# Order of the first attention phase in a fused attention and two-FFN kernel: weight conversions, bias tables and reciprocal products placed behind the latest maximum

## The chip, the cores and the metric

One core of one Trainium2 chip runs the whole program. The metric is the device time of one execution in microseconds (us). Half a per cent of it is about 4.9 us. The engines have short names: PE is TensorE (PEld its weight loads), DVE is VectorE, ACT is ScalarE, POOL is GpSimd, SP is SyncE, whose queue issues every DMA here.

## The reference, cut to what matters

Attention over 4 batches, 8 heads, 576 positions, head dimension 64, with a causal mask and a bias from a running sum of `s`; then two feed-forward networks over the 2304 tokens. All data are float32, and the kernel keeps that precision by splitting operands into a high and a low part.

```python
scores = scale * np.matmul(q, k.transpose(0, 1, 3, 2))
cum = np.cumsum(np.maximum(s, 0.0), axis=-1)
bias = -(cum[:, :, :, None] - cum[:, :, None, :])
scores = np.where(causal, -1000000000.0, scores + np.minimum(bias, 0.0))
scores = scores - np.max(scores, axis=-1, keepdims=True)
attn = np.exp(scores)
attn = attn / (np.sum(attn, axis=-1, keepdims=True) + 1e-09)
x = np.matmul(attn, v)                      # then tokens x 512
h = x @ w_in;  x = (h - np.tanh(h)) @ w_out          # d_ff 2048
x = ((x @ w1) * (x @ w2) @ w3) @ w_out2              # d_ff 1024
```

## The kernel before, in words

The kernel has three phases. Only the first is touched: attention, with the first half of the first network (feature blocks 0 to 7) laid between its steps as filler for PE. The rest of the first network and the second network follow.

**Pairs and steps.** Attention works on pairs of heads. `Pair` objects are numbered in the order in which they run: p0 to p3 are the first 256 queries ("A") of batch 0's four head pairs, p4 to p7 the other 320 queries ("B") of the same; from p8 on come the batches 1 to 3. An A pair has one unit of work, a B pair has three (B1, B2, B3). A loop over steps `k`, from -2 on, calls what the table `when` holds for each step, in the order given by a small number; `at(k, order, fn)` fills the table (lines 486 to 513). Unit `j` of a pair scores at its step, takes its row maximum and its exponentials one step later, is transposed 5 (A of batch 0) or 7 steps later, and so on. p0, p1, p2, p3 score at steps 0, 2, 4, 6; p4 at 8, 10, 12, p5 at 14, 16, 18, and so on to p7 at 26, 28, 30; p8 at 32. In steps 0 to 11 three idle matmuls (`warm`, line 197) stand at each step.

**Batch 0.** Here the bias is added by PE: `scores` (line 208) follows the score matmuls with matmuls of two small tables, `rel0` and `rel1`, made by `relative` (line 568) on DVE from the running sum; five column ranges are made, for the five chunks of queries, and all five stand ahead of the first maximum. `minimum` (line 231) takes the row maxima on DVE (L241) and scales them by -0.125 (L245); `exps` (line 257) computes the exponentials on ACT from the PSUM banks (L270, L271). In unit B3 two chunks end: chunk 2 (all in B3's banks) and chunk 4 (512 columns in B2's banks, 64 in B3's), so B2's two banks stay taken until chunk 4 is through ACT.

**Banks.** Scores, transposes and products share a pool of five PSUM banks (`ps_a`). PE's order is the program's own (`manual_schedule`); a score matmul that finds no bank stops PE until ACT has read one.

**Products.** `invert` makes reciprocals of the row sums; they go by PE transpose (`turn`), ACT (`store`), a DMA to DRAM (L329) and two broadcast DMAs back (`spread`, L335) to a tile `rb`; `finish` (line 344) multiplies the attention product by it on DVE (L348) into `xy`, from which `xhl`, the network's input, is split by ACT (L63) and DVE (L64). The network's first block may start when p3 is finished: `fin` (line 510) is its step, 15 for p3.

**Weights.** Weight tiles arrive as 64-bit numbers and are turned to float32 by three DVE instructions (`plain`, lines 78 to 89: L82, L85, L87), split by ACT (L63) and POOL (L64). `conversions` (line 353) loads and converts them one after the other through two raw tiles; the first two loads are issued at the start, the first conversions stand in steps 0 and 3, later ones every 2.2 steps (line 601), and each from the third on waits for the latest score matmul (`after_pe`, a semaphore wait). `parked` (line 368) does the same from step 36 on for the other half of the weights.

**Order.** On DVE, ACT, POOL and SP each engine runs its instructions in one fixed order, which the scheduler of the framework sets from the program's order, priorities and its own timing model. So a wait of one instruction holds all behind it on the engine.

## Time and profile before

| | |
|---|---|
| median of 3 runs | 974.52 us (971.75 to 977.34) |
| profiled execution, its own time | 970.3 us |
| its span, first to last instruction | 968.5 us |
| mean granted PE clock | 0.989 |
| PE busy | 935.1 us (97%) |
| PEld / DVE / ACT / POOL busy | 808.1 / 558.3 / 418.3 / 258.3 us |
| PE idle in 0 to 60 us / after 340 us | 11.4 us / 11.8 us |

The busy table says how long each engine worked, not what set the end. The two rows on idle time are the lengths of those stretches less PE's busy time in them. The view of waits by engine, the timeline of one engine and the table of stretches with the granted clock tell where PE stood still, and at which clock it worked after.

### The profile page before, as it was taken

Reading aid. Unit: us, or ns where it says so; the run is one execution under the profiler, and the core shown is the slowest. Engines: PE = TensorE matmul, PEld = TensorE weight load, DVE = VectorE, ACT = ScalarE, POOL = GpSimd, SP = SyncE. Lnnn points to the kernel's source line nnn. Section 1 sums busy time; section 2 is a strip of 40 time slices with the busy share of each in tenths; the row PEclk is TensorE's granted clock in tenths of the full one; section 3 lists DMA queues with packets and bytes.
Section 4 is the critical chain, followed back from the end, with each engine's and each line's share of the span. In section 5 each row is a group of like instructions: output and inputs, shape, how many; then the busy total and the mean of one; then the engine's idle time right before and its main releaser. Section 6 shows DMA issues by size and latency. Waiting matters only on the chain.

```text
span 968.5 us, 16343 instructions
## 1 busy us (share of the span) xinstructions
PE 935.1 (97%) x5953; PEld 808.1 (83%) x5953; DVE 558.3 (58%) x1311; ACT 418.3 (43%) x1029; POOL 258.3 (27%) x254
## 2 busy tenths in 40 slices
PE   8799999899999999999999999989999999999997
PEld 4466776688788789998888888978899999999997
DVE  8565556677667776776977566785322712342221
ACT  4565777767676654333433333332222412331220
POOL 3123766455555510000000000023222501340220
PEclk9898999999999999999999999999999999999999
DMA  6544353554444522489573563484366737664611
GB/s 200 164 137 149 123 193 135 178 184 153 162 142 147 178 102 97 162 299 362 212 262 140 193 217 131 134 283 157 101 196 196 206 101 205 196 173 151 197 55 66
DMA packets 67711, 165.66 MB, mean 171 GB/s; under 512 B 7504, under 2 KB 22000, under 8 KB 65584
## 3 DMA queue, kind: packets, MB, share of 16 engines
q1 hardware_dynamic: 67632, 164.62, 51.7%
q8 instruction: 47, 0.77, 0.3%
q14 instruction: 32, 0.26, 0.1%
HBM read 127.74 MB, written 36.86 MB: 170 GB/s over the span
## 4 chain that ended last, share of the span: by engine, by line
PE 81%; DMA 3%; issue 3%; POOL 3%; DVE 2%; ACT 2%; SPq 0%; POOLq 0%; ACTq 0%; DVEq 0%
PE W L813 10%; PE hb L111 9%; PE yb L111 9%; PE h L111 9%; PE y L416 8%; PE o L829 5%; PE Y L813 5%; PE q L829 5%; PE w3o L111 5%; PE pv L311 4%; PE s_B L214 4%; PE pt_B L285 3%; PE V L813 2%; POOL pr L193 1%; DMA raw_w<-in_w3t 1%
## 5 line engine op out<-in xcount | busy, mean ns | idle before, releaser
L111 PEld LDWEIGHTS h<-xhl,win 128*128 128x128 f32 x864 | 107.0, 189 | 21.7 <-issue 10.7
L111 PE MATMUL h<-xhl,win 128*128 128x256 f32 x864 | 121.7, 287 | 1.3 <-DVE th L448 0.6
L111 PE MATMUL hb<-x,win 128*128 128x512 f32 (+1 forms) x480 | 104.6, 367 | 0.0
L111 PE MATMUL yb<-ghb,wout 128*128 128x512 f32 (+1 forms) x320 | 96.1, 367 | 0.4 <-ACT ghb L63 0.4
L111 PEld LDWEIGHTS hb<-x,win 128*128 128x128 f32 x480 | 83.9, 188 | 15.0
L193 POOL TENSOR_SCALAR pr<-cb,cq 128x384 f32<-128x384 f32 (+1 forms) x48 | 88.2, 1852 | 2.9 <-DMA cb<-cum_d 2.1
L416 PE MATMUL y<-gh,wout 128*128 128x256 f32 x576 | 86.8, 290 | 0.0
L274 ACT ACTIVATE pr<-pr,nm 128x128 f32<-128x128 f32 (+2 forms) x120 | 71.3, 596 | 22.4 <-DVE nm L252 21.8
L64 POOL TENSOR_TENSOR B11hl<-xy,B11hl 128x768 fp32r<-128x768 f32 x3 | 5.6, 1863 | 279.8 <-ACT B11hl L63 279.8
L416 PEld LDWEIGHTS y<-gh,wout 128*128 128x128 f32 x576 | 73.8, 191 | 5.2 <-issue 4.0
L885 POOL TENSOR_TENSOR c<-c,c 128x384 f32<-128x384 f32 x24 | 25.8, 1074 | 171.8 <-DVE c L869 171.8
L111 PEld LDWEIGHTS yb<-ghb,wout 128*128 128x128 f32 x320 | 58.2, 188 | 10.5 <-ACT ghb L63 0.6
L214 PE MATMUL s_B<-qk 64*96 64x512 f32 (+2 forms) x256 | 57.5, 513 | 9.4 <-ACT pr L270 6.8
L829 PE MATMUL o<-p,w3s 128*128 128x384 f32 x288 | 61.4, 335 | 1.0 <-ACT p L63 1.0
L111 PE MATMUL yb<-glb,wout 128*128 128x512 f32 (+1 forms) x160 | 58.5, 368 | 0.4 <-DVE glb L64 0.4
L252 DVE CUSTOM_DVE_ANT_0 pr<-s_B,pr 96x512 f32<-96x512 f32 (+1 forms) x72 | 44.9, 639 | 19.9 <-PE s_B L214 18.6
L285 PE MATMUL pt_B<-ident,pr 96*128 96x96 f32 (+1 forms) x384 | 52.5, 260 | 0.3 <-ACT pf_A L294 0.3
L829 PEld LDWEIGHTS o<-p,w3s 128*128 128x128 f32 x288 | 50.8, 188 | 1.5 <-ACT p L63 1.3
L829 PE MATMUL q<-p,w3s 128*128 128x384 f32 x288 | 50.9, 335 | 0.1
L829 PEld LDWEIGHTS q<-p,w3s 128*128 128x128 f32 x288 | 50.0, 188 | 0.4 <-DVE pp L882 0.4
L294 ACT COPY pf_B<-pt_B 128x512 f32<-128x512 f32 (+2 forms) x72 | 35.8, 497 | 30.3 <-PE pt_B L285 29.5
L416 PE MATMUL y<-gl,wout 128*128 128x256 f32 x288 | 45.7, 281 | 2.7 <-POOL gl L64 2.7
(169 smaller groups left out, 1871.8 us busy)
## 6 DMA issues: line engine op xcount, KB each, us to landing
S<-wg_d SPq DMA_DIRECT2D x96, 256.0 KB
A<-wg_d SPq DMA_DIRECT2D x72, 256.0 KB
qk<-in_qk SPq DMA_DIRECT2D x16, 576.0 KB
raw_win<-in_w_in SPq DMA_DIRECT2D x16, 512.0 KB
raw_wout<-in_w_out SPq DMA_DIRECT2D x16, 512.0 KB
raw_w<-in_w SPq DMA_DIRECT2D x16, 512.0 KB
wg_d<-pks SPq DMA_DIRECT2D x8, 1024.0 KB
raw_w<-in_w3t SPq DMA_DIRECT2D x16, 512.0 KB
```

The source lines that it names most:

```text
L111: i = nc.tensor.matmul(ps, a, b, start=first and n == 0, stop=last and n == 2, skip_group_check=skip)
L193: nc.gpsimd.tensor_scalar(out=t[:pw, e, :w], in0=p.cb[:pw, e, :w], scalar1=c, scalar2=0.0, op0=ALU.add, op1=ALU.min)
L214: latest[0] = nc.tensor.matmul(ps[e][:PW[i], o:o + k1 - k0], x[:, 0, CH0[i]:CH0[i] + PW[i]], x[:, 1, k0:k1], start=(i, k0, k1, o) == UNITS ...
L252: nc.vector.tensor_tensor_reduce(out=t[:pw, k0:k1], in0=ps[:pw, o:o + k1 - k0], in1=t[:pw, k0:k1], scale=-0.125, scalar=nm[:pw, 5:6] if k0 ...
L274: nc.scalar.activation(t[:pw, :], t[:pw, :], AF.Exp, bias=m, scale=-1.0, accum_out=p.sums[:pw, e, c:c + 1])
L285: nc.tensor.transpose(pt[:, at:at + pw], p.pr[i][:pw, e, KC0[kj]:KC0[kj] + P], ident[:pw, :pw])
L294: (nc.vector.tensor_copy if j == "B2" and not p.first else nc.scalar.copy)(pf[:, :at], pt[:, :at])
L311: nc.tensor.matmul(p.pv[D * e:D * e + D, c:p.nq], p.vs[:, e, kj], pf[:, beg:end], start=z == 0, stop=z == len(todo) - 1, skip_group_check= ...
L416: nc.tensor.matmul(o, wout[f][:, z, P * c:P * c + P], x, start=f == 0 and n == 0 and c % 2 == 0, stop=f == F1 - 1 and n == 2, skip_group_c ...
L813: nc.tensor.matmul(ps[:, :T], w[:, x, P * j:P * j + P], b[:, y, j], start=first and j == n == 0, stop=last and j == 1 and n == 2, skip_gro ...
L829: nc.tensor.matmul(os_[c][:, :T], w3s[f][:, a, P * c:P * c + P], p[:, b], start=f == 0 and n == 0, stop=f == NG - 1 and n == 2, skip_group ...
L885: nc.gpsimd.tensor_mul(c12, c12, c22)
```

## The change

It touches the first phase only.

1. `in_turn` is new: it orders an instruction behind another on the same engine, without a semaphore. `latest` remains the latest score matmul; the new `least` is the latest instruction of a row maximum (L249 of the new kernel, or the fused one for later batches).
2. The first DVE instruction of each conversion stands in turn behind `least`, and waits no more for a score matmul.
3. The first two raw loads are no longer issued at the start: `conversions` is first called at step 1, then every second step, 18 times to step 35; so loads are issued at steps 1 and 3, behind the latest score matmul, and the first two conversions stand at steps 5 and 7.
4. The bias tables are ordered behind `least`; the first two chunks' are still made before any maximum, the others now behind one.
5. The products of `finish` are ordered behind `least`; for A pairs of batch 0 they stand one step later (`fin` + 5), so the network's first block may start at step 16.
6. Where batch 0 takes maxima and exponentials, the chunks of a unit come in reverse: in B3 chunk 4 before chunk 2, in A chunk 1 before chunk 0.

```diff
+    def in_turn(i, behind):
+        if behind is not None:
+            tc.add_manual_dep(i.ins, behind.ins.name, mybir.DependencyInfo(mybir.DependencyClass.NoSync, mybir.DependencyReason.SCHED_ONLY))
...
-        after_pe(i, behind)
+        in_turn(i, behind)
...
-        latest, paces = [None], []
+        latest, least, paces = [None], [None], []
...
-                for i, k0, k1, o in UNITS[j]:
+                for i, k0, k1, o in reversed(UNITS[j]):
...
-                        nc.vector.tensor_scalar(out=nm[:pw, :, c:c + 1], in0=nm[:pw, :, c:c + 1], scalar1=-0.125, scalar2=None, op0=ALU.mult)
+                        least[0] = nc.vector.tensor_scalar(out=nm[:pw, :, c:c + 1], in0=nm[:pw, :, c:c + 1], scalar1=-0.125, scalar2=None, op0=ALU.mult)
...
-                    nc.vector.tensor_tensor_reduce(
+                    least[0] = nc.vector.tensor_tensor_reduce(
...
-            for i, k0, k1, o in UNITS[j]:
+            for i, k0, k1, o in reversed(UNITS[j]) if p.first else UNITS[j]:
...
-                    nc.vector.tensor_mul(xy[:, p.hp, c:c + z - q], p.pv[:, q - p.q0:z - p.q0], p.rb[:, r:r + z - q])
+                    in_turn(nc.vector.tensor_mul(xy[:, p.hp, c:c + z - q], p.pv[:, q - p.q0:z - p.q0], p.rb[:, r:r + z - q]), least[0])
...
-                raws.append(load_raw(*todo[m][2:], nc.sync if m < 2 else nc.scalar, pin=fs[0] == 0))
-                if m < 2:
-                    yield
+                raws.append(load_raw(*todo[m][2:], behind=latest[0]))
+                yield
...
-                d[f] = convert(raws.pop(0), n, behind=latest[0] if m > 1 else None)
+                d[f] = convert(raws.pop(0), n, behind=least[0])
...
-                park(raws.pop(0), n, wf_d[m], f2, latest[0])
+                park(raws.pop(0), n, wf_d[m], f2, least[0])
...
-            fin = ke + lag + (4 if p.first and p.early else 3)
+            fin = ke + lag + (5 if p.first and p.early else 3)
...
-        next(conv)
-        next(conv)
...
-            nc.vector.tensor_scalar(out=hi, in0=cum[:, :w], scalar1=base, scalar2=None, op0=ALU.subtract)
+            in_turn(nc.vector.tensor_scalar(out=hi, in0=cum[:, :w], scalar1=base, scalar2=None, op0=ALU.subtract), least[0])
...
-            if k >= 0 and convs < 2 * F1 and 5 * k >= 11 * convs:
+            if convs < 2 * F1 + 2 and k >= 1 + 2 * convs:
                 at(k, 5.8, next, conv, None)
                 convs += 1
-            if convs == 2 * F1 and k >= 36 and k % 6 == 0:
+            if convs == 2 * F1 + 2 and k >= 36 and k % 6 == 0:
```

What this does to the order of the engines is shown at three places. The number after a tile's name tells tiles of one kind apart; it is not the same in the two kernels.

DVE from the bias tables to the first maximum, before (`rel` are the tables, `cvt` the converted weights, `nm` the maxima of p0 and p1):

```order
L574 SCALAR_TENSOR_TENSOR rel_139<-cum,rel_139 32x512
L574 SCALAR_TENSOR_TENSOR rel_138<-cum,rel_138 32x576
L574 SCALAR_TENSOR_TENSOR rel_139<-cum,rel_139 32x384
L82 TENSOR_SCALAR cvt_win_179<-raw_win_126 128x512
L82 TENSOR_SCALAR cvt_wout_246<-raw_wout_128 128x512
L85 SCALAR_TENSOR_TENSOR cvt_win_179<-raw_win_126,cvt_win_179 128x512
L85 SCALAR_TENSOR_TENSOR cvt_wout_246<-raw_wout_128,cvt_wout_246 128x512
L87 SCALAR_TENSOR_TENSOR cvt_win_179<-raw_win_126,cvt_win_179 128x512
L87 SCALAR_TENSOR_TENSOR cvt_wout_246<-raw_wout_128,cvt_wout_246 128x512
L241 TENSOR_REDUCE nm_188<-s_A_162 128x1 x2
L241 TENSOR_REDUCE nm_188<-s_A_163 128x1 x2
```

The same place now (the lines are those of the changed kernel, L245 and L249 for the maximum):

```order
L574 TENSOR_SCALAR rel_134<-cum 32x128
L574 TENSOR_SCALAR rel_134<-cum 32x256
L575 SCALAR_TENSOR_TENSOR rel_134<-cum,rel_134 32x128
L575 SCALAR_TENSOR_TENSOR rel_134<-cum,rel_134 32x256
L245 TENSOR_REDUCE nm_175<-s_A_158 128x1 x2
L245 TENSOR_REDUCE nm_175<-s_A_159 128x1 x2
L249 TENSOR_SCALAR nm_175<-nm_175 128x2 x2
L574 TENSOR_SCALAR rel_135<-cum 32x512
L575 SCALAR_TENSOR_TENSOR rel_135<-cum,rel_135 32x512
```

Three of the five tables moved behind the first and the second maximum, and both conversions behind the third and the fourth.

DVE at the maxima of p4's unit B3, before (`xy<-pv_544` is the product of p3):

```order
L241 TENSOR_REDUCE nm_410<-s_B_0_510 128x1
L241 TENSOR_REDUCE nm_410<-s_B_0_510 96x1
L241 TENSOR_REDUCE nm_410<-s_B_1_511 128x1
L241 TENSOR_REDUCE nm_410<-s_B_1_511 96x1
L348 TENSOR_TENSOR xy<-pv_544,rb_507 128x256
L245 TENSOR_SCALAR nm_410<-nm_410 128x2
L243 TENSOR_TENSOR nm_410<-nm_410 96x2
L245 TENSOR_SCALAR nm_410<-nm_410 96x2
```

The same place now (`xy<-pv_473` is the product of p2; that of p3 comes ten rows further on):

```order
L245 TENSOR_REDUCE nm_392<-s_B_0_492 96x1
L245 TENSOR_REDUCE nm_392<-s_B_0_492 128x1
L245 TENSOR_REDUCE nm_392<-s_B_1_493 96x1
L245 TENSOR_REDUCE nm_392<-s_B_1_493 128x1
L247 TENSOR_TENSOR nm_392<-nm_392 96x2
L249 TENSOR_SCALAR nm_392<-nm_392 128x2
L86 TENSOR_SCALAR cvt_win_525<-raw_win_418 128x512
L249 TENSOR_SCALAR nm_392<-nm_392 96x2
L352 TENSOR_TENSOR xy<-pv_473,rb_439 128x256
```

The product of p3 no longer stands between the maxima and their scaling, but the first instruction of a conversion does.

ACT at the exponentials of p4's B3, before:

```order
L63 CAST xhl_2_592<-xy 128x256
L63 CAST xhl_3_595<-xy 128x256
L271 ACTIVATE pr_2_468,sums_425<-s_B_0_510,nm_410 128x384
L271 ACTIVATE pr_2_468,sums_425<-s_B_1_511,nm_410 128x384
L270 ACTIVATE pr_4_407,sums_425<-s_B_0_460,nm_410 96x512
L271 ACTIVATE pr_4_407,sums_425<-s_B_0_510,nm_410 96x64
L270 ACTIVATE pr_4_407,sums_425<-s_B_1_461,nm_410 96x512
```

The same place now:

```order
L274 ACTIVATE pr_4_389,sums_407<-s_B_0_442,nm_392 96x512
L275 ACTIVATE pr_4_389,sums_407<-s_B_0_492,nm_392 96x64
L274 ACTIVATE pr_4_389,sums_407<-s_B_1_443,nm_392 96x512
L275 ACTIVATE pr_4_389,sums_407<-s_B_1_493,nm_392 96x64
L275 ACTIVATE pr_2_450,sums_407<-s_B_0_492,nm_392 128x384
L275 ACTIVATE pr_2_450,sums_407<-s_B_1_493,nm_392 128x384
L63 CAST xhl_2_600<-xy 128x256
```

Chunk 4, which reads B2's banks, now comes ahead of chunk 2, and the split of `xhl`, which waits for the products, behind both.

On PE only the network's matmuls move: `h` of block 0, feature block 0, starts one step (16 for 15) later, and the units after it follow at the new spacing; the attention matmuls keep their order.

## Rows read from the trace of the kernel before

**Rows 1.** The page: span, and busy time of each engine.

```profile
span 968.5 us, 16343 instructions
...
PE 935.1 (97%) x5953; PEld 808.1 (83%) x5953; DVE 558.3 (58%) x1311; ACT 418.3 (43%) x1029; POOL 258.3 (27%) x254
```

**Rows 2.** PE's timeline (start, duration, instruction xcount [idle before <-releaser]).

```profile
9.05 0.23 PE L229 MATMUL s_A<-maskb,identb 128*128 128x128 bf16 x1
...
15.76 0.92 PE L214 MATMUL s_A<-qk 64*128 64x128 f32 x6 [1.62 <-ACT pr L271]
...
19.67 0.93 PE L214 MATMUL s_A<-qk 64*128 64x128 f32 x8
...
36.10 0.21 PE L229 MATMUL s_B<-maskb,identb 128*96 128x64 bf16 x1
...
37.04 1.10 PE L214 MATMUL s_B<-qk 64*96 64x512 f32 x2
...
43.46 2.02 PE L214 MATMUL s_B<-qk 64*96 64x512 f32 x2 [5.33 <-ACT pr L270]
...
59.84 2.07 PE L214 MATMUL s_B<-qk 64*96 64x512 f32 x4 [1.90 <-ACT pf_B L294]
...
77.33 1.10 PE L214 MATMUL s_B<-qk 64*96 64x512 f32 x2 [0.52 <-ACT pf_B L294]
79.94 2.02 PE L214 MATMUL s_B<-qk 64*96 64x512 f32 x2 [1.52 <-ACT pr L270]
...
101.52 1.21 PE L214 MATMUL s_A<-qk 64*128 64x128 f32 x8 [2.42 <-ACT pr L270]
```

**Rows 3.** Stretches: us, PE busy (xcount), granted clock, DMA share, GB/s.

```profile
43.50:48.40 4.90, 4.90 (x15) 0.50 0.35 105
45.50:49.50 4.00, 4.00 (x22) 0.58 0.49 152
79.90:86.20 6.30, 6.26 (x21) 0.50 0.52 188
103.40:106.90 3.50, 3.50 (x18) 0.51 0.00 0
```

**Rows 4.** DVE's timeline, tables, conversions and first maximum.

```profile
5.19 1.90 DVE L573 TENSOR_SCALAR rel<-cum 32x128 fp32r<-32x128 f32 x5
7.12 2.60 DVE L574 SCALAR_TENSOR_TENSOR rel<-cum,rel 32x128 fp32r<-32x128 f32 x5
...
12.23 0.69 DVE L87 SCALAR_TENSOR_TENSOR cvt_wout<-raw_wout,cvt_wout 128x512 uint32<-128x512 uint32 x1
12.84 1.15 DVE L241 TENSOR_REDUCE nm<-s_A 128x1 f32<-128x128 f32 x4
13.90 0.52 DVE L245 TENSOR_SCALAR nm<-nm 128x2 f32<-128x2 f32 x2
```

**Rows 5.** DVE's timeline, the maxima of p4's B3.

```profile
37.76 1.27 DVE L241 TENSOR_REDUCE nm<-s_B 128x1 f32<-128x384 f32 x4
40.75 0.42 DVE L348 TENSOR_TENSOR xy<-pv,rb 128x256 f32<-128x256 f32 x1 [1.73 <-DMA rb<-rd]
...
41.35 0.17 DVE L245 TENSOR_SCALAR nm<-nm 96x2 f32<-96x2 f32 x1
```

**Rows 6.** ACT's timeline, exponentials of p4's B3.

```profile
41.52 0.57 ACT L271 ACTIVATE pr<-s_B,nm 128x384 f32<-128x384 f32 x1
...
42.64 0.67 ACT L270 ACTIVATE pr<-s_B,nm 96x512 f32<-96x512 f32 x1
```

**Rows 7.** SP's timeline, two of its DMA issues.

```profile
36.26 1.11 SPq L335 DMA_DIRECT2D rb<-rd  x2
...
45.51 0.33 SPq L167 DMA_DIRECT2D qk<-in_qk  x1
```

**Rows 8.** DVE's timeline, a conversion beside a subtraction of POOL.

```profile
22.02 1.62 DVE L85 SCALAR_TENSOR_TENSOR cvt_wout<-raw_wout,cvt_wout 128x512 uint32<-128x512 uint32 x1
```

**Rows 9.** POOL's timeline at the same time.

```profile
21.82 1.27 POOL L64 TENSOR_TENSOR win<-cvt_win,win 128x512 fp32r<-128x512 f32 x1 [6.28 <-ACT win L63]
```

## What the change should do to the time

> **What bounds the kernel now.** The page comes first: PE works 935.1 of 968.5 us [rows 1], so only the 33 us in which it stands still, and the time in which it runs at the lower clock, can be won without less work; the change removes no matmul. The view of PE's waits and its timeline tell where: beside the start, the first 110 us hold a wait of 1.62 us for the exponentials of p0, one of 5.33 at the scores of p5, then 1.90 (p6), 0.52 and 1.52 (p7) and 2.42 (p8) [rows 2]. In the row of p6 a second wait is hidden: its four matmuls take 2.07 us, while two take 1.10 at p7 and could take so in pairs; I count 1.0 more. The table of stretches shows what follows: from 43.5 to 48.4, 79.9 to 86.2 and 103.4 to 106.9 PE was granted half of its clock, 1.2 instead of 2.4 GHz [rows 3]. It fell after stillness of 5.33 us, of 0.52 and 1.52, and of 2.42; after 1.62 and after 1.90 it did not. Work at half clock costs half of the busy time of the stretch: 2.45, 3.1 and 1.7 us.
>
> The timelines of DVE and ACT tell why PE waited. At the start DVE makes five bias tables (4.5 us) and two conversions, until 12.92, while p0's scores are done at 9.28; only at 12.84 does the first maximum begin [rows 2, 4]. At p5 the four reductions of p4's B3 are done at 39.0, but the scaling follows at 41.35, behind the product of p3, which waited for its reciprocals until 40.75 [rows 5]; then chunk 2 takes ACT until 42.64, and only then chunk 4 frees a bank of B2 [rows 6], for which PE has waited since 38.1.
>
> The sum below goes against the profiled execution, 970.3 us, 1.8 above its span. The median of the three runs, 974.52, lies 4.2 above it; the gain is taken off that median.
>
> **A, the start (tables, first conversions, raw loads).** Nothing is removed; 1472 of 1856 table columns, 3.6 of the 4.5 us, and both conversions (9.72 to 12.92, 3.2 us) move behind maxima. The first two tables end at some 6.6, so p0's maximum begins at 9.0, when the first half of its scores is there, and takes 1.5 [rows 4]. Then on DVE: a table of 512 columns 1.2, a wait of 0.3 for p0's sums, p1's maximum 1.5, the other two tables 2.3, p2's maximum 1.5: 17.3. Three of p2's four exponentials later, 1.1, the fourth score has its bank at 18.4; before, it began at 19.67 [rows 2]. So the 1.62 us go, and about 0.9 us come back before the fourth score. I take 1.3 (0 if the tables in between cost more, 3.5 if p0's head start came through). The raw loads, issued some 6 and 10 us later, are first used behind p2's and p3's maxima, near 17.3 and 21; the only large load that the rows isolate, 576 KB issued at 45.51, had moved by about 49.5 (4.0 us at 152 GB/s) [rows 3, 7], so issues near 9 and 13 are in time. On SP the two loads no longer stand ahead of the `v` loads of p0 and p1 and the store of the running sum, and now come behind the `qk` loads of p3 and p4; the reciprocals' DMAs still come after them, so nothing there gets later that PE waits for.
>
> **B, the wait at p5.** PE reaches p5's second score, 38.1 before, at 36.85. The scores of B3 end at 36.31 less 1.3 [rows 2], 35.0; the reductions follow within half of 1.27, to 35.65; three small ones of 0.15 to 0.17 and the first third of a conversion (half of 0.69, an estimate) end at 36.25; chunk 4 is now first on ACT, 0.67, and frees the bank at 36.9 [rows 5, 6]. The wait of 5.33 shrinks to 0.1: 5.2 (bounds 1.0, if the load in front comes 4 us late, and 5.3). Of products and splits, which now come behind, none is due before the network's start.
>
> **C, the half clock at p5.** With no wait there it does not fall: 2.45 (bounds 0 and 2.5).
>
> **D, a new wait at the network's start.** Block 0 now starts at step 16. Its fourth operand, `xhl` of p3, needs p3's product, which stands behind p5's first maximum, and behind that on DVE come two conversions and two reductions of p5's B2. From p5's first maximum, near 38.1, DVE has to do: two reductions (some 0.6 each, like those at 37.76 with 384 columns, a little longer with 512), p3's product and p2's split at 0.42 each, five conversion instructions of up to 0.69, again two reductions, and the split itself: 38.1 + 1.3 + 0.8 + 3.0 + 1.3 + 0.4 = 44.9, and 45.8 with one conversion beside POOL (below). PE gets there near 43, an estimate: some 6 us after p5's second score, for the fifty or so matmuls in between at 0.1 to 0.2 us. I take 2.9 lost (0.5 if the two conversions come at their quickest and PE later, 4.5 if a load is late too). p3's reciprocals themselves are in time: their broadcasts were issued at 36.26 to 37.37 and read at 40.75, 3.4 us later, and now are issued no later, and read near 41 [rows 5, 7].
>
> A row bears on this: the second instruction of a conversion takes 1.62 us where it begins 0.2 us into a subtraction of POOL that lasts until 23.09, and 0.69 alone (its third one, same size) [rows 4, 8, 9]; 0.93 more. I count one such meeting. The Trainium skill, "SBUF — State Buffer", section "SBUF: two separate sides", says that such a pair takes an exclusive lock, the loser blocked until the other's whole instruction is done. By that rule 23.09 + 0.69 = 23.78 would be the end, and the trace has 23.64, so they agree within 0.15; a meeting at the very start would cost 1.27, and the sum with it 0.3 us less gain.
>
> **E, p6.** Of 1.90 and 1.0 I keep 1.1, since chunk 4 no longer comes behind chunk 2's two exponentials (1.12 from 41.52 to 42.64): 1.8 (0.5 and 2.9).
>
> **F, p7.** The 0.52 for a copy of ACT stays; the 1.52 for chunk 4 falls by 1.12, and PE comes later by the network's matmuls that the step's shift puts in front: 1.5. Without it the half clock of 79.9 to 86.2 goes: 3.1 (0 and 3.1).
>
> **G, p8.** 2.42 less 1.1: 1.1, and half of the 1.7 at half clock, 0.85, since 1.3 us lies between the waits that lowered the clock and those that did not.
>
> **H, later.** In batches 1 to 3 the products and the parked conversions stand in turn too, so products come a little later; I take 1.0 lost (2 lost to 1 won), with no row for it. After the first 340 us nothing moves: same work, shifted.
>
> Sum: 1.3 + 5.2 + 2.45 - 2.9 + 1.8 + 1.5 + 3.1 + 1.1 + 0.85 - 1.0 = 13.4, so 956.9 on the profiled execution's scale and 974.5 - 13.4, **961.0**, for the median.
>
> **Rivals.**
> - *The clock falls all the same.* For: it fell after only 0.52 and 1.52. Against: not after 1.62 and 1.90. Then C, F and G give back 6.4: 967.5.
> - *POOL's port.* DVE's order now has conversions in twos, the second beside the subtraction of the first. Four meetings more of 0.93 on the path: 3.7, 964.7. By the Trainium skill's lock (the page and section named under D) four meetings would cost up to 1.27 each, 5.1 in all.
> - *Loads in front of a maximum.* A conversion stands between the two scalings of B3. Its load can be issued only when the conversion two before it has left its raw tile. If it lands 4 us late, B and C shrink by 6.7 and, at p6 to p8 likewise, most of E to G: some 12 us gone, 973.
> - *Slower: DVE is held by every conversion.* The semaphore on the scores is gone, so DVE runs into conversions whose loads have not landed; each then holds the maximum behind it. Eleven conversions from the third to step 31: at 1.2 us each the gain is gone, at 2.0 us, half of the load's 4.0, 22 are lost: 983. For it: SP issues in order, behind reciprocals that wait for ACT. Against: two raw tiles, and 4 to 5 us between conversions of one tile.
> - *The order does not hold*, as it has no semaphore: DVE's instructions stand as asked in the program, so I give it nothing of its own.
>
> **How the numbers follow.** Forecast 0.55, clock 0.17, port 0.10, loads 0.12, slower 0.06. Half a per cent, 4.9 us, is what a measurement of this kernel tells from none, so faster means below 969.6. Faster: 0.55 + 0.10 + 0.13 of the clock's, 0.78. The same: 0.04 + 0.12, 0.16. Slower 0.06. The range goes down to 957 (A, D and H at their better ends give some 4 us more) and up to 971.5, which leaves out the slower case, two thirds of the loads' and a little of each tail.
>
> **What would show it.** Right: the first maximum begins near 9; the fourth score near 18.4; no wait over 1 us at p5, and full clock from 40 to 110; a wait near 43 for `xhl`; PE done with p8's scores some 14 us earlier. Wrong: DVE idle in front of a conversion for a DMA; a stretch at half clock in the first 110 us; waits after 110 us that were not there.

## The result, and the profile after

The changed kernel takes **963.75 us** (median of 4 runs, 960.15 to 965.21), beside 973.54 us for the kernel before (4 runs on the same chip): ratio **0.9889**, 95% interval 0.9848 to 0.9930. Run again with five rounds on another occasion it gave 964.00 beside 974.11 us, 0.9905 (0.9874 to 0.9935). The forecast was 961.0, its range 957.0 to 971.5, and "faster".

The profiled execution took 960.15 us, 10.1 less than the one of before (970.3). Its page, span and busy time, answers to [rows 1]; PE's busy time fell by 4.3 us with no matmul gone, since less of it ran at half clock:

```profile
span 958.4 us, 16338 instructions
...
PE 930.8 (97%) x5953; PEld 804.1 (84%) x5953; DVE 568.3 (59%) x1311; ACT 417.0 (44%) x1029; POOL 256.7 (27%) x254
```

PE's timeline (start, duration, instruction, count, idle time before it and what ended that) answers to [rows 2]:

```profile
17.49 0.92 PE L218 MATMUL s_A<-qk 64*128 64x128 f32 x6 [0.48 <-ACT pr L275]
...
22.31 1.10 PE L218 MATMUL s_B<-qk 64*96 64x512 f32 x4
...
33.98 1.42 PE L218 MATMUL s_B<-qk 64*128 64x384 f32 x8 [2.68 <-ACT rt L331]
...
38.73 1.10 PE L218 MATMUL s_B<-qk 64*96 64x512 f32 x2 [0.54 <-ACT pr L274]
...
41.70 1.80 PE L218 MATMUL s_B<-qk 64*96 64x512 f32 x4
...
47.76 0.51 PE L115 MATMUL h<-xhl,win 128*128 128x256 f32 x2 [1.79 <-DVE xhl L64]
...
52.53 1.77 PE L218 MATMUL s_B<-qk 64*96 64x512 f32 x4 [0.57 <-ACT pf_B L298]
...
65.81 0.55 PE L289 MATMUL pt_B<-ident,pr 128*128 128x128 f32 x4 [1.04 <-DVE cq L588]
...
71.65 1.95 PE L218 MATMUL s_B<-qk 64*96 64x512 f32 x4 [0.46 <-ACT pr L274]
...
89.49 0.92 PE L218 MATMUL s_A<-qk 64*128 64x128 f32 x6 [0.42 <-ACT pr L274]
...
131.67 0.85 PE L289 MATMUL pt_B<-ident,pr 128*128 128x128 f32 x5 [1.66 <-DVE xy L352]
...
194.32 1.65 PE L115 MATMUL h<-xhl,win 128*128 128x256 f32 x12 [1.27 <-DVE th L451]
...
256.13 1.64 PE L115 MATMUL h<-xhl,win 128*128 128x256 f32 x12 [1.62 <-DVE th L451]
```

The waits of p5 (5.33 before, 0.54 now), p6 (1.90, 0.57), p7 (0.46 is left) and p8 (2.42, 0.42) shrank as forecast. Part of them is hidden, as at p6 before: the four matmuls of a score take 1.10 us where both banks are free (22.31), but 1.80 at 41.70, 1.77 at 52.53 and 1.95 at 71.65, 0.7 to 0.85 us more each. Six rows are new: 2.68 us at p4's B3 for ACT's copy `rt`, 1.79 us for `xhl` at the network's start, 1.04 us at 65.81 for a small table of DVE (not followed further), 1.66 us at 131.67, and 1.27 and 1.62 us for `th`, the network's hidden layer on DVE, at 194 and 256. The table of stretches (PE busy, granted clock, DMA) shows full clock from 40 to 110 and half behind the wait at 131.67, where [rows 3] had three stretches at half:

```profile
40.00:110.00 70.00, 65.56 (x482) 1.00 0.54 171
132.00:138.00 6.00, 5.50 (x27) 0.50 0.20 79
```

Where the 10.1 us came from is read at matmuls that have the same work ahead of them in both kernels (end = start plus duration in PE's timeline):

| end of | before | after | gain so far | gain since the row above |
|---|---|---|---|---|
| p4's B2 scores | 31.69 | 28.92 | 2.77 | 2.77 |
| p4's B3 scores | 36.31 | 36.37 | -0.06 | -2.83 |
| p5's B3 scores | 55.15 | 50.59 | 4.56 | 4.62 |
| p8's products, near 127 before | 126.74 | 114.57 | 12.17 | 7.61 |
| the span | 968.5 | 958.4 | 10.1 | -2.1 |

So the start's gain was lost at p4's B3, the stretch from there to p8's products brought 12.2, and 2.1 were lost later. The two losses can be followed on DVE and ACT. DVE's timeline, answering to [rows 4, 5]:

```profile
5.94 0.68 DVE L575 SCALAR_TENSOR_TENSOR rel<-cum,rel 32x128 fp32r<-32x128 f32 x2
7.83 1.15 DVE L245 TENSOR_REDUCE nm<-s_A 128x1 f32<-128x256 f32 x4 [1.22 <-PE s_A L233]
...
31.16 0.42 DVE L352 TENSOR_TENSOR xy<-pv,rb 128x256 f32<-128x256 f32 x1 [2.38 <-DMA rb<-rd]
...
34.45 1.27 DVE L245 TENSOR_REDUCE nm<-s_B 96x1 f32<-96x512 f32 x2
35.98 1.28 DVE L245 TENSOR_REDUCE nm<-s_B 96x1 f32<-96x64 f32 x4 [0.26 <-PE s_B L233]
...
37.78 0.41 DVE L352 TENSOR_TENSOR xy<-pv,rb 128x256 f32<-128x256 f32 x1
...
46.83 0.88 DVE L64 TENSOR_TENSOR xhl<-xy,xhl 128x256 fp32r<-128x256 f32 x1
```

ACT's timeline of the same stretch, and at 126:

```profile
31.61 0.41 ACT L63 CAST xhl<-xy 128x256 fp32r<-128x256 f32 x1 [3.68 <-DVE xy L352]
32.21 0.62 ACT L63 CAST win<-cvt_win 128x512 fp32r<-128x512 f32 x1 [0.19 <-DVE cvt_win L91]
33.15 0.62 ACT L63 CAST wout<-cvt_wout 128x512 fp32r<-128x512 f32 x1 [0.32 <-DVE cvt_wout L91]
33.67 0.25 ACT L331 COPY rt<-pri 4x128 f32<-4x128 f32 x1
...
126.35 2.82 ACT L199 ACTIVATE pr<-cb,cq 128x256 f32<-128x256 f32 x6 [2.98 <-DMA cb<-cum_d]
```

**The first loss.** The first two tables end at 6.6 and the first maximum begins at 7.83, as meant. But at 31.16 p1's product has waited 2.38 us for its reciprocals, and B2's maximum comes behind it only at 34.45, B3's at 35.98. (p2's product, at 37.78, does stand behind B3's, as meant.) Behind the same product stand the rest of two conversions, and behind these on ACT the casts at 31.61, 32.21 and 33.15; only then comes the copy of p3's transposed sums (33.67), which frees the bank for which PE waits until 33.98. The cause is in the code: `least` is set by the scaling (L249), and B2's part of chunk 4 has a maximum but no scaling, since that is done in B3. So "behind the latest maximum" means behind B1's there.

**The second loss.** SP's and POOL's timelines:

```profile
117.57 0.33 SPq L104 DMA_DIRECT2D wf_d<-park_win  x1
...
119.25 0.44 SPq L181 DMA_DIRECT2D cb<-cum_d  x1
```

```profile
45.83 1.60 POOL L64 TENSOR_TENSOR wout<-cvt_wout,wout 128x512 fp32r<-128x512 f32 x1 [2.55 <-ACT wout L63]
...
116.25 1.29 POOL L64 TENSOR_TENSOR park_win<-cvt_win,park_win 128x512 fp32r<-128x512 f32 x1 [0.47 <-ACT park_win L63]
```

The store of the first parked weight (`wf_d<-park_win`) waits for POOL's subtraction until 117.54 and stands in SP's queue ahead of the load `cb` that the next pairs' bias needs. ACT and POOL begin on `cb` at 126.35 and 126.49; the split, the product and PE come late behind ACT. In the kernel before the same two DMAs stood the other way round:

```profile
129.34 0.38 SPq L177 DMA_DIRECT2D cb<-cum_d  x1
...
134.01 0.34 SPq L100 DMA_DIRECT2D wf_d<-park_win  x1
```

### The profile page after: what moved, and what is told of

It reads as the page before. It is cut to its first block, busy times and chain, and to the rows that moved or that the text cites. A ratio compares the mean times of both kernels' runs of the same rounds, so it can differ in the third digit from the quotient of the medians.

```text
span 958.4 us, 16338 instructions
## 1 busy us (share of the span) xinstructions
PE 930.8 (97%) x5953; PEld 804.1 (84%) x5953; DVE 568.3 (59%) x1311; ACT 417.0 (44%) x1029; POOL 256.7 (27%) x254
## 4 chain that ended last, share of the span: by engine, by line
PE 78%; DVE 7%; DMA 6%; issue 4%; POOL 3%; ACT 2%; SPq 0%; ACTq 0%; POOLq 0%; DVEq 0%
PE W L814 10%; PE hb L115 10%; PE yb L115 9%; PE h L115 8%; PE y L419 8%; PE o L830 5%; PE Y L814 5%; PE q L830 5%; PE s_B L218 4%; PE pv L315 3%; PE pt_B L289 3%; PE w3o L115 3%; PE V L814 2%; DMA raw_w<-in_w3t 2%; POOL pr L197 2%
## 5 line engine op out<-in xcount | busy, mean ns | idle before, releaser
L115 PE MATMUL w3o<-wo,w3b 128*128 128x512 f32 x192 | 45.9, 401 | 2.6 <-DVE xy L717 2.5
L289 PEld LDWEIGHTS pt_B<-ident,pr 96*128 96x128 f32 (+1 forms) x384 | 41.2, 143 | 7.2 <-issue 3.2
```

What stands on the lines that cost most here:

```text
L115: i = nc.tensor.matmul(ps, a, b, start=first and n == 0, stop=last and n == 2, skip_group_check=skip)
L289: nc.tensor.transpose(pt[:, at:at + pw], p.pr[i][:pw, e, KC0[kj]:KC0[kj] + P], ident[:pw, :pw])
```

## The experiments

All times are medians beside the kernel before on the same chip, with the ratio and its 95% interval. A difference between two changed kernels "by the ratios" is worked out from two of them. The interval of every version below overlaps or touches one of the change's two (0.9848 to 0.9930, 0.9874 to 0.9935), so such differences are likely rather than certain. Diffs are against the changed kernel unless said otherwise.

### The change once more

> The changed kernel itself once more, with 5 rounds beside the next three. Theory: its PE waits about 2.7 us at p4's B3 for the copy of p3's transposed sums in every execution, and whether the clock falls there differs from execution to execution (it did not in the first profile; it did behind the same wait in two experiments, 35 to 45 us): a ratio of 0.989 to 0.992, and profiles that differ by 3 to 5 us at p5. Rival: the clock does not fall there, the profile repeats within 1 us.

964.00 us, 0.9905 (0.9874 to 0.9935). The profiled execution took 959.9, the second lowest of a spread of 959.88 to 968.53. PE's timeline:

```profile
33.17 1.42 PE L218 MATMUL s_B<-qk 64*128 64x384 f32 x8 [1.92 <-ACT rt L331]
```

The wait is there again, 1.92 us, and the clock held. The ratio is where the theory had it, but the two profiles are only 0.8 us apart at p5's B3 (49.77 against 50.59), as the rival had it. The clock did not fall in either profile of this kernel; in those of the next kernels it did, in the same place (the table further down).

### Without the reversed chunks

```diff
-                for i, k0, k1, o in reversed(UNITS[j]):
+                for i, k0, k1, o in UNITS[j]:
...
-            for i, k0, k1, o in reversed(UNITS[j]) if p.first else UNITS[j]:
+            for i, k0, k1, o in UNITS[j]:
```

> The changed kernel with the chunks of batch 0 in their natural order again, in the scalings and in the exponentials; all else of the change stays. Theory: the last chunk first is what frees the bank that the next pair's scores wait for, so each wait for B2's bank at p5 to p8 comes back by about the 1.1 us of chunk 2's two exponentials, and the clock may fall once or twice again: 3 to 8 us slower than the changed kernel, about 967 to 972. Rival (the order of products and tables alone did it): no wait over 1 us at p5 to p8 and no difference over 1 us.

965.39 us, 0.9945 (0.9925 to 0.9965): by the ratios 3.9 to 5.5 us slower than the change, inside the theory's range. PE's timeline and a stretch:

```profile
34.41 2.28 PE L218 MATMUL s_B<-qk 64*128 64x384 f32 x8 [2.75 <-ACT rt L331]
...
56.40 1.45 PE L218 MATMUL s_B<-qk 64*96 64x512 f32 x4 [1.57 <-ACT pr L274]
```

```profile
36.00:46.00 10.00, 10.00 (x40) 0.50 0.60 178
```

The wait at p6 is 1.57 us (0.57 with the reversal) and ended by chunk 4's exponentials; that is the theory's one microsecond. At p8 it is 0.64 (0.42 with the reversal), and at p5 (here at half clock) and p7 no wait of the scores came back. The half clock from 34 to 47 belongs to the wait at p4's B3, which the chunks don't touch: 2.9 of the 5.5 us that this profile is behind the change's at p8's products (120.06 against 114.57) were lost by p5's B3 (53.46 against 50.59), and only the other 2.6 behind it.

### Reversal alone, products alone

Two parts by themselves, on the kernel before. The first has the two reversed loops and nothing else; the second this, with `least` set as in the change:

```diff
-                    nc.vector.tensor_mul(xy[:, p.hp, c:c + z - q], p.pv[:, q - p.q0:z - p.q0], p.rb[:, r:r + z - q])
+                    in_turn(nc.vector.tensor_mul(xy[:, p.hp, c:c + z - q], p.pv[:, q - p.q0:z - p.q0], p.rb[:, r:r + z - q]), least[0])
...
-            fin = ke + lag + (4 if p.first and p.early else 3)
+            fin = ke + lag + (5 if p.first and p.early else 3)
```

> The kernel before with one part of the change alone: in batch 0 the last chunk first, in the scalings and in the exponentials. Theory: at p6, p7 and p8 the bank of B2 comes free some 1.1 us sooner and the clock holds there, as in the sum's E, F and G; at p5 the product of p3 still holds the scalings, so the wait and the half clock there stay for the most part: 4 to 8 us faster than before. Rival (the parts only work together): within 2 us of before.

> The kernel before with another part of the change alone: products in turn behind the latest maximum, finished a step later in batch 0. Theory: at p5 the wait falls from 5.3 to between 2 and 4 us, since chunk 4 still comes behind chunk 2's exponentials, and the clock may still fall; p6 to p8 stay as before: 1 to 4 us faster than before. Rival (without the chunk order nothing is won, and xhl of p3 comes later): within 1 us of before, or slower by up to 2.

Reversal alone: 966.42 us, 0.9924 (0.9900 to 0.9949), some 7.4 us faster than before, inside its range. Products alone: 968.34 us, 0.9948 (0.9926 to 0.9970), some 5.1 us, more than the 1 to 4 expected. PE's timeline of the one, then of the other:

```profile
16.22 1.65 PE L214 MATMUL s_A<-qk 64*128 64x128 f32 x6 [2.26 <-ACT pr L271]
...
45.43 2.02 PE L214 MATMUL s_B<-qk 64*96 64x512 f32 x2 [4.26 <-ACT pr L270]
```

```profile
40.08 1.10 PE L218 MATMUL s_B<-qk 64*96 64x512 f32 x2 [1.52 <-ACT pr L274]
...
76.00 2.06 PE L218 MATMUL s_B<-qk 64*96 64x512 f32 x4 [2.13 <-ACT pr L274]
```

With the reversal alone the wait at p5 stays, 4.26 us: the product of p3 still stands in front of the scaling. With the products alone it falls to 1.52 us, less than I expected, and the clock held there. So B is the work of the product order, and the reversal takes off about one microsecond more; each part alone gives about half of the whole gain or more, so they overlap. At p6 to p8 the reversal alone shortened the waits (0.77, 0.40 and 1.84 us instead of 1.90, 1.52 and 2.42), but PE had half clock again from 81.1 to 84.4 and from 101.6 to 104.9, so this part of the theory failed. With the products alone the waits there stayed, 2.09, 2.13 and 2.15 us, as expected.

### Products free again

```diff
-                    in_turn(nc.vector.tensor_mul(xy[:, p.hp, c:c + z - q], p.pv[:, q - p.q0:z - p.q0], p.rb[:, r:r + z - q]), least[0])
+                    nc.vector.tensor_mul(xy[:, p.hp, c:c + z - q], p.pv[:, q - p.q0:z - p.q0], p.rb[:, r:r + z - q])
...
-            fin = ke + lag + (5 if p.first and p.early else 3)
+            fin = ke + lag + (4 if p.first and p.early else 3)
```

> The changed kernel with the products of Y and reciprocals no longer ordered behind the latest maximum, and finished a step earlier as before; all else stays. Theory: a product that waits for its reciprocals holds the reductions of p4's B3 or the scalings behind it again, so part of the wait at p5 is back, 1 to 5 us with 1 to 2.5 us of half clock, while the wait of 1.79 us for xhl at the network's start goes: 0 to 5 us slower than the changed kernel. Rival (the chunk order alone cured p5): PE waits under 1 us at p5, the 1.79 us go, and the kernel is 1 to 2 us faster.

963.27 us, 0.9924 (0.9905 to 0.9942), by the ratios 1.9 to 3.4 us slower than the change, inside the theory's range, but not for the reason given. The scheduler put p3's product behind both scalings by itself, so PE's wait at p5 is 0.54 as in the change and this run doesn't test the theory; the products alone, above, do. A loss that the change doesn't have lies near 113 us, where PE waited 2.00 us for the `xhl` of the network's second block and then had half clock. The last experiment shows the same.

### The start as before

```diff
-                raws.append(load_raw(*todo[m][2:], behind=latest[0]))
+                raws.append(load_raw(*todo[m][2:], pin=True))
...
-                d[f] = convert(raws.pop(0), n, behind=least[0])
+                d[f] = convert(raws.pop(0), n, behind=least[0] if m > 1 else None)
...
+        next(conv)
+        next(conv)
...
-            in_turn(nc.vector.tensor_scalar(out=hi, in0=cum[:, :w], scalar1=base, scalar2=None, op0=ALU.subtract), least[0])
+            nc.vector.tensor_scalar(out=hi, in0=cum[:, :w], scalar1=base, scalar2=None, op0=ALU.subtract)
...
-            if convs < 2 * F1 + 2 and k >= 1 + 2 * convs:
+            if convs < 2 * F1 and k >= 0 and 5 * k >= 11 * convs:
...
-            if convs == 2 * F1 + 2 and k >= 36 and k % 6 == 0:
+            if convs == 2 * F1 and k >= 36 and k % 6 == 0:
```

> The changed kernel with its start as before: two raw loads at the start, two conversions and all five tables ahead of the first maximum, and the conversions at their old spacing; all else stays. Theory: the gain at the start, 2.2 to 2.8 us by p3 and p4, is taken up at p4's B3, where PE waits 2.68 us for the copy of p3's transposed sums whichever time it comes: 0 to 1 us slower, PE some 2.5 us later until 30 us and level with the changed kernel from p4's B3 on. Rival (the start's gain goes through to the end): 2.2 to 2.8 us slower.

963.50 us, 0.9919 (0.9903 to 0.9936): by the ratios 1.4 to 2.9 us slower. That lies between theory and rival and settles nothing. Its profile shows why the start is worth more than one pair of profiles tells; PE's timeline:

```profile
16.26 1.65 PE L218 MATMUL s_A<-qk 64*128 64x128 f32 x6 [2.65 <-ACT pr L275]
```

PE stood still for 2.65 us there (1.62 in [rows 2]), and then had half clock until about 23. It was not level from p4's B3 on, as the theory had it: the end of that score was 4.25 us behind the change's (40.62 against 36.37).

### p3's sums in another bank

```diff
-            p.pt = ps_a.tile([P, 512], F32, tag="s", name=f"pri{p.n}")
+            p.pt = ps_h.tile([P, 512], F32, tag="h", name=f"pri{p.n}") if p.n == 3 else ps_a.tile([P, 512], F32, tag="s", name=f"pri{p.n}")
```

> The changed kernel with the transposed sums of p3 in a bank of the hidden layer instead of one of the scores', so that the scores of p4's B3 wait for no copy; all else stays. Theory: DVE is what sets the end there, held by p1's product until its reciprocals land near 31 us, so PE's wait moves from p4's B3 to p5's scores: 0 to 1.5 us faster than the changed kernel. Rival (the copy alone is the cause): the wait of 2.7 us goes and nothing takes its place, 2.7 us faster, and up to 5 with the clock.

963.91 us, 0.9905 (0.9869 to 0.9940), the same as the change. PE's timeline:

```profile
34.87 1.05 PE L218 MATMUL s_B<-qk 64*128 64x384 f32 x6 [2.47 <-ACT pf_A L298]
```

Two of the eight matmuls got through; the other six waited 2.47 us for the next bank, which a copy of ACT behind the same casts sets free. So neither the theory (that the wait moves to p5) nor the rival: it is not the bank, but ACT's queue behind p1's product.

### B2's maximum counts

```diff
-                        nc.vector.tensor_reduce(out=nm[:pw, e, c:c + 1], in_=p.banks[j][e][:pw, o:o + k1 - k0], op=ALU.max, axis=mybir.AxisListType.X)
+                        least[0] = nc.vector.tensor_reduce(out=nm[:pw, e, c:c + 1], in_=p.banks[j][e][:pw, o:o + k1 - k0], op=ALU.max, axis=mybir.AxisListType.X)
```

> The changed kernel with one more rule: the first part of chunk 4's maximum (B2, which has no scaling) counts as a latest maximum too, so p1's product and the second conversion stand behind it instead of ahead of it; all else stays. Theory: p1's product, 2.38 us of waiting for its reciprocals, held B2's maximum and by the casts behind it the copy that PE waits for at p4's B3; without it that wait falls under 0.7 us, the start's gain of 2.2 to 2.8 us goes through and the clock holds: 2 to 5 us faster than the changed kernel. Rival (DVE has the same work and the wait only moves to p5 or to the network's start): within 1 us.

**959.98 us**, 0.9859 (0.9826 to 0.9891), 4.0 below the change's median in the same set of runs; its six runs reach from 956.89 to 961.93, the change's eight from 959.88 to 968.53. DVE's, ACT's and PE's timelines:

```profile
28.75 1.28 DVE L245 TENSOR_REDUCE nm<-s_B 96x1 f32<-96x512 f32 x2 [0.62 <-PE s_B L233]
...
31.47 0.42 DVE L352 TENSOR_TENSOR xy<-pv,rb 128x256 f32<-128x256 f32 x1 [1.10 <-DMA rb<-rd]
```

```profile
30.17 0.26 ACT L331 COPY rt<-pri 4x128 f32<-4x128 f32 x1 [1.60 <-PE pri L326]
```

```profile
32.77 1.05 PE L218 MATMUL s_B<-qk 64*128 64x384 f32 x6 [0.52 <-ACT pf_A L298]
```

B2's maximum now begins at 28.75 instead of 34.45, p1's product waits behind it, ACT copies p3's sums at 30.17 instead of 33.67, and PE's wait is 0.52 instead of 2.68. The theory holds, though not all of the start's gain goes through: 2.65 us at p4's B2, 1.51 at its B3.

### The later batches as before

```diff
...
-        in_turn(i, behind)
+        (after_pe if wait else in_turn)(i, behind)
...
-        w = convert(raw, name, pool.tile([P, 2, DM], F32R, tag="park", name=f"park_{name}", bufs=1), behind=behind)
+        w = convert(raw, name, pool.tile([P, 2, DM], F32R, tag="park", name=f"park_{name}", bufs=1), behind=behind, wait=True)
...
-                    in_turn(nc.vector.tensor_mul(xy[:, p.hp, c:c + z - q], p.pv[:, q - p.q0:z - p.q0], p.rb[:, r:r + z - q]), least[0])
+                    in_turn(nc.vector.tensor_mul(xy[:, p.hp, c:c + z - q], p.pv[:, q - p.q0:z - p.q0], p.rb[:, r:r + z - q]), least[0] if p.first else None)
...
-                park(raws.pop(0), n, wf_d[m], f2, least[0])
+                park(raws.pop(0), n, wf_d[m], f2, latest[0])
```

> The changed kernel with the products in turn for batch 0 alone, and the conversions that are parked with the semaphore on the latest scores again as before; all else stays. Theory: what the change lost behind 110 us (a wait of 1.66 us at 131.7 and 6.9 us at half clock) comes from these two orders in the later batches: 2 to 3 us faster than the changed kernel, about 961, and no half clock near 132. Rival (the loss is a matter of when transfers meet there, not of these orders): no difference over 1 us, the wait near 131 stays.

960.01 us, 0.9886 (0.9868 to 0.9904). By the ratio that is no difference to the change (0.9889 and 0.9905). PE's timeline and two stretches:

```profile
34.68 2.28 PE L218 MATMUL s_B<-qk 64*128 64x384 f32 x8 [2.48 <-ACT rt L331]
```

```profile
36.00:44.00 8.00, 8.00 (x31) 0.50 0.49 169
128.00:140.00 12.00, 10.46 (x74) 0.89 0.51 148
```

Its profile was 3.0 us behind the change's at p5's B3 (53.55 against 50.59): 0.9 of it was there at p4's B2 already, the rest came with the half clock behind the wait at p4's B3. It won them back later: at p8's products it was 9.4 us ahead of before and at products near 365 still 9.9, while the change fell from 12.2 to 9.5. The wait near 131 is gone; the half clock in the second stretch stands behind another wait, 1.54 us for POOL at 135.70, which the change's second profile has too (1.53).

All fourteen profiles bear it out. In the eight with the parked conversions in turn the store goes ahead of `cb`, which is issued 3.4 to 5.0 us behind the end of p8's products, and seven of them have a wait for `xy` like the one at 131.67, 1.04 to 2.48 us. In the six with the semaphore, the kernel before among them, `cb` goes first, 2.6 to 3.2 us behind the products, and none has that wait. The two waits for `th` behind it go too: this profile has 0.51 us near 256 and none near 194. So H is real in the profiles, and the medians neither show nor exclude it. Of the two orders that this run undoes only one does anything: with the products of the later batches free or in turn, every engine's order is the same, so it is the parked conversions.

### Both together

The two diffs above in one kernel.

> The rule of the run before (B2's maximum counts) together with the later batches as before the change (products free there, parked conversions with the semaphore). Theory: the two losses of the change add up and both go: 4 to 8 us faster than the changed kernel, 953 to 957. Rival (each shifts the meetings of transfers near 130 us anew): no better than the run before by over 1 us.

**957.93 us**, 0.9840 (0.9807 to 0.9874), the fastest of the series: 6.1 below the change's median in the same set, and all its five runs (955.65 to 959.60) lie below all eight of the change there. SP's timeline, and PE's:

```profile
115.10 0.38 SPq L181 DMA_DIRECT2D cb<-cum_d  x1
...
119.78 0.33 SPq L104 DMA_DIRECT2D wf_d<-park_win  x1
```

```profile
170.22 0.74 PE L419 MATMUL y<-gl,wout 128*128 128x256 f32 x4 [1.97 <-POOL gl L64]
```

`cb` is again issued ahead of the store, and the wait near 131 is gone. What is left is a wait of 1.97 us for POOL at 170.22 with half clock behind it; the kernel before has the same wait, 1.95 us at 185.84, with full clock behind it. The theory's 4 to 8 us holds for the pair; that the second part adds to the first is 2.1 us by the medians, inside their intervals.

### The old start, with B2's maximum counted

The diff of "The start as before" and that of "B2's maximum counts" in one kernel.

> The changed kernel with B2's maximum counted as a latest maximum, and its start as before: two raw loads at the start, two conversions and five tables ahead of the first maximum. Theory: with the wait at p4's B3 gone the gain of the start goes through, so here 2 to 4 us are lost against the same kernel with the new start (959.98 in its runs, ratio 0.986). Rival (the start's gain is taken up by the next wait all the same): within 1 us of it.

963.23 us, 0.9888 (0.9856 to 0.9920): 2.8 us slower than with the new start by the ratios (0.9859), as the theory says, though the intervals overlap. PE's timeline, and a stretch of it and of the reversal alone, which has the old start too:

```profile
16.22 0.92 PE L218 MATMUL s_A<-qk 64*128 64x128 f32 x6 [2.26 <-ACT pr L275]
```

```profile
18.00:20.00 2.00, 2.00 (x15) 1.00 0.41 165
```

```profile
18.00:20.00 2.00, 2.00 (x10) 0.50 0.41 166
```

Both stood still for 2.26 us and went on at the same 16.22; the first kept full clock, though it had stood still for 0.96 us more at 7.9, and the second fell to half.

### Block 0 a step earlier

Against the fastest version:

```diff
-            fin = ke + lag + (5 if p.first and p.early else 3)
+            fin = ke + lag + (4 if p.first and p.early else 3)
```

> B2's maximum counted, the later batches as before, and batch 0's products finished a step earlier again (they stay in turn), so that the network's first block starts a step earlier. Theory: the split of p3 comes ahead of the reductions of p5's B2 on DVE, and the wait of about 2 us for it at the network's start shrinks to under 1.2: 1 us faster than with the later step (957.93, ratio 0.984), at most 2. Rival (the network asks a step earlier, so the wait stays or grows): the same or up to 2 us slower.

964.17 us, 0.9898 (0.9873 to 0.9924), 5.6 us slower by the ratios than with the later step; neither the theory nor the rival had it so. The wait at the network's start did shrink (2.24 to 0.37 us), but PE's timeline has another later, with half clock from 116 to 119:

```profile
115.75 0.70 PE L115 MATMUL h<-xhl,win 128*128 128x256 f32 x2 [1.79 <-DVE xhl L64]
```

So the step that I priced only as a cost is worth more than it costs. Some 3 us of it lie here, where the second block with the early step asks for its input too soon. The rest is not explained: this profile had half clock behind p6's scores (54.5 to 57.8) and near 150 (150.1 to 153.4) too. Why the kernel before, with the early step, has no such wait was not tried.

### One table over all profiles

The end of p4's B2 and B3 scores in each profiled execution (us), and whether PE had half clock between:

| start | kernel | B2 | B3 | half clock up to there |
|---|---|---|---|---|
| old | before | 31.69 | 36.31 | no |
| old | reversal alone | 34.80 | 39.34 | 16 to 23 |
| old | products alone | 32.20 | 36.74 | no |
| old | start as before | 34.79 | 40.62 | 16 to 23 |
| old | the same, B2 counts | 33.63 | 38.20 | no |
| new | the change | 28.92 | 36.37 | no |
| new | the change again | 28.88 | 35.56 | no |
| new | no reversal | 29.28 | 38.42 | from 34 |
| new | later as before | 29.82 | 38.70 | from 35 |
| new | other bank | 29.19 | 36.90 | from 37 |
| new | B2 counts | 29.04 | 34.80 | no |
| new | both together | 30.01 | 34.87 | no |
| new | products free | 30.17 | 35.76 | no |
| new | block 0 earlier | 29.50 | 35.54 | no |

The old start ends B2's scores at 33.4 on average (five executions), the new one at 29.4 (nine). So the start is worth about 4 us up to there, not the 2.8 of the two first profiles, since the profiled execution of the kernel before had the quickest start of all with the old order. Two of the five had half clock from 16 to 23; the other three end at 32.5 on average, which leaves 3.1 us.

## Why the prediction was right, and where its terms were off

The direction, the range and the mechanism at p5 were right, that at p6 to p8 in part; 961.0 was 2.75 us too low. That it is not further off is partly luck, since errors of both signs meet in the sum. The measured 963.75 even lies nearer to the 964.7 of "POOL's port", but not by that rival's mechanism (see below). Of the signs named, the first maximum came at 7.83 (9 forecast), p5 had no wait over 1 us and the clock was full from 40 to 110; the wait for `xhl` began at 45.97 (43 forecast), and p8's scores ended 12.3 us earlier, not 14 (102.73 before, 90.41 now). Waits behind 110 us that were not there before, a sign of "wrong", came as well. Set against the two profiled executions (13.4 forecast, 10.1 measured):

- **A, the start**: 1.3 forecast, 2.77 measured, 1.5 to 2.8 in the nine executions with the new start against the one of before, and about 4 against the mean of the old start (3.1 against those at full clock). Undersized: I worked from one execution of before, whose start was its quickest.
- **A term that was missing: -2.83.** Under B the text says "Of products and splits, which now come behind, none is due before the network's start". That sentence failed. p1's product comes ahead of B2's maximum, since that one is not counted as a latest maximum, and holds it and ACT's copies. One line in the code cures it, and the time shows it: 4.0 us.
- **B, C and D, p5 up to its B3**: 5.2 + 2.45 - 2.9 = 4.75 forecast, 4.62 measured. The wait became 0.54, the clock held. B took 0.6 us for small instructions whose figures in the text add up to 0.8; they took 0.7 (37.18 to 37.87). D's wait was 1.79, not 2.9: from p5's first maximum DVE needed 7.4 us (40.32 to 47.71, 7.7 forecast), but PE came later than I thought, 7.2 us behind p5's second score (38.73 to 45.97), not some 6. That the sum is so close is luck: the three terms as measured, 4.79 + 2.45 - 1.79, give 5.45, and 0.7 of what is missing is the hidden wait at 41.70. The split in question is the row at 46.83, 0.88 us, beside POOL's subtraction from 45.83 to 47.43 (0.41 alone). That it was a meeting with POOL fits the Trainium skill, "SBUF — State Buffer", section "SBUF: two separate sides", the rule named in the prediction (the one that comes second is blocked until the other's whole instruction is done): POOL's end and 0.41 give 47.84, and the split ended at 47.71. What the step behind D brings (the last experiment) I had not priced.
- **E, F and G**: 1.8 + 4.6 + 1.95 = 8.35 forecast, 7.61 measured. The waits and the half clock went as forecast, but the reversal, the cause that E to G name, is not all of it. In the profile without it the same stretch, from p5's B3 to p8's products, still gained 4.99 of the 7.61 us: p6's wait came back, those of p7 and p8 hardly did, while with the products alone all three stood at over 2 us. So the new places of tables and conversions, which E to G don't price, bring part of it. No run has the conversions' places by themselves, so how much is theirs stays open.
- **H, later**: -1.0 forecast with no row for it, -2.1 measured. The mechanism is named now: a store that waits for POOL ahead of a load in SP's queue, in every profile with the parked conversions in turn and in no other. My text had the products in the later batches among its causes; they don't move at all.

Of the rivals, "the clock falls all the same" was half right, in another place: it falls behind p4's B3 in some executions of the change's kind. "Loads in front of a maximum" and "DVE held by every conversion" were not seen; the longest wait of DVE for a raw load between 16 and 48 us was 0.91, at 27.15. "POOL's port" was seen in three splits (1.49, 1.10 and 0.88 us instead of 0.41), and only the last of them ended a wait of PE.

Open: how often the clock falls behind p4's B3 in the unprofiled runs of the change. Its spread (959.88 to 968.53) leaves room for the 2 to 3 us that this cost in the profiles, which is an argument and not shown.

## What to carry to other kernels

When an instruction is ordered "behind the latest X", list every X in the program and look whether each one sets the mark; the one that sets none is where the order fails, and here it cost 2.8 us of a gain of 2.8. Look also at what stands behind the held instruction on the other engines: PE's wait was named after a copy of ACT, and moving its bank did nothing, while moving a product on DVE did. And compare starts over several executions before sizing a gain there: one profile can be the quickest of its kind.

## What the runs showed of the hardware

Whether PE's clock fell behind a short stillness was not settled by its length. At the start, 2.26 us were followed by half clock in one execution and by full clock in another, 1.62 and 2.30 by full and 2.65 by half. At p4's B3, 1.92 and 2.68 us were followed by full clock, 2.47, 2.48 and 2.75 by half. At the network's start, 1.79 and 2.24 us were followed by full clock, 1.86, 2.09 and 2.57 by half; at its second block 1.79 us was followed by half. At the network's matmul `y<-gl` between 170 and 186 us, 1.95 us was followed by full clock in two kernels, 1.96 and 1.97 by half in three. In the two kernels that differ only in the later batches, p5's B3 ended at 53.55 where the clock fell and at 50.59 and 49.77 where it held: 3.0 to 3.8 us, of which 0.9 had been there at p4's B2. I had read one execution and taken its clock as the kernel's; in these runs waits of this size went both ways, so such a term wants a chance and not a yes or no.
